# Attention decode kernel on one core: the closing wait for the two output stores moved from SyncE to ScalarE

**Chip and metric.** One core of one Trainium2 chip. The metric is the device time of one execution in microseconds (us), as a median of several executions.

## The reference

A grouped-query attention block with a full key and value cache, for 32 sequences of 4 new positions:

```python
B, Sq, D = 32, 4, 1024
Hq, Hkv, Sk, Dh = 32, 4, 2048, 128
q = (x @ wq).reshape(B, Sq, Hq, Dh).transpose(0, 2, 1, 3)
k = repeat(k_cache, Hq // Hkv, axis=1);  v = repeat(v_cache, Hq // Hkv, axis=1)
p = softmax(einsum("bhqd,bhkd->bhqk", q, k) * Dh ** -0.5)
o = einsum("bhqk,bhkd->bhqd", p, v)
return o.transpose(0, 2, 1, 3).reshape(B, Sq, Hq * Dh) @ wo      # all bfloat16
```

The output is 128 rows by 1024 columns of bfloat16, 256 KB. The inputs are 151 MB.

## The kernel before

Everything up to the last matmul is loads and compute that the change does not touch. What counts is the end. The result lies in PSUM, where the last matmuls write it, in three column ranges; VectorE copies the first and the third to SBUF, ScalarE the second. Two DMAs store it: SyncE issues the left half, ScalarE the right half.

```python
for j, eng in enumerate(("dve", "act", "dve")):
    copy(eng, *COLS[j], j)
for j, (n0, n1, waits) in enumerate(((0, NA, (0,)), (NA, D, (1, 2)))):
    p.dma(("sp", "act")[j], lambda e, n0=n0, n1=n1: e.dma_start(out_flat[:, n0:n1], y_sb[:, n0:n1]),
          [("oe", i) for i in waits], ("out", j), f"s_o{j}")
# ... cut ...
with nc.Block() as block:          # line 499: each engine's stream; closes with a barrier of all engines
    # ... cut: the five engines' streams ...

for j in range(2):                 # after the block
    s, n = p.at["out", j]
    nc.sync.wait_ge(sems[s], n)    # line 523
```

Each store has its own semaphore (`s_o0`, `s_o1`; 114 and 115 in the trace), a counter that is updated 16 times as the store lands: from 360.096 to 360.273 us, and from 360.562 to 360.744. No other instruction of the program waits for the stores: SyncE leaves the block's barrier at 359.709 us, the later store lands at 360.744.

## Time and profile before

| | kernel before |
|---|---|
| time, median of 3 runs | 362.17 us (362.14 to 362.23) |
| span in the profile, first to last instruction | 360.8 us |
| data moved | 151.66 MB, 420 GB/s |
| later store: issue, last landing | 358.976, 360.744 us |
| closing wait on SyncE | 360.761 to 360.789 us |

The span covers the program's own instructions. The time has 1.3 us more (362.09 in the profiled run, for a span of 360.789). What follows the program has no row in any view of the profile, but the trace still holds the times at which semaphores were updated. Semaphore 2 is named by no instruction of the program, and no record says what updates it. Its updates after the block's barrier, from 359.995 to 362.219 us, I number 1 to 18: they come as two groups of nine, which I call passes. Where I say "the record of semaphore 2", this list is meant.

### The profile page before, as it was taken

The numbers are of one execution on the slowest core, as the hardware profiler recorded it, in microseconds if no ns is written. First come the engines' busy times: TensorE is split into PE (matmuls) and PEld (weight loads), VectorE is DVE, ScalarE is ACT, GpSimd is POOL, SyncE is SP. The second block draws the span as 40 slices with busy tenths as digits, with TensorE's granted clock in tenths as the row PEclk, the third lists the DMA queues.
The fourth block names the chain that finished last, engine by engine and source line by source line (L and its number), as shares of the span: only waits on it lengthen the run. The fifth ranks groups of instructions, "written<-read, shape, count | busy, mean of one in ns | idle before, by whom it ended". The sixth has DMA issues, their size and how long they took to land. (4 is left out here: it accounts for less than half of the span.)

```text
span 360.8 us, 6251 instructions
## 1 busy us (share of the span) xinstructions
PE 307.6 (85%) x3034; PEld 147.0 (41%) x2340; DVE 269.5 (75%) x171; ACT 102.8 (28%) x110; POOL 165.9 (46%) x262
## 2 busy tenths in 40 slices
PE   1988788999999999988999888888888898889896
PEld 1002000445444554444444444443333444448721
DVE  0018799999899888879999888888888888865601
ACT  1014222333333333333333333323222233333100
POOL 8002055255555555554455444455555554444100
DMA  8999999999999999999999999999999999999996
GB/s 323 432 434 431 421 429 432 429 417 432 428 423 425 432 431 427 424 432 431 423 427 432 430 423 429 431 432 423 429 431 432 423 429 431 429 425 431 413 417 243
DMA packets 12251, 151.66 MB, mean 420 GB/s; under 512 B 1360, under 2 KB 2128, under 8 KB 2768
## 3 DMA queue, kind: packets, MB, share of 16 engines
q1 hardware_dynamic: 12096, 151.39, 99.1%
q8 instruction: 6, 0.10, 0.1%
q10 hardware_dynamic: 144, 0.13, 0.1%
q14 instruction: 5, 0.04, 0.0%
HBM read 151.26 MB, written 0.26 MB: 420 GB/s over the span
## 5 line engine op out<-in xcount | busy, mean ns | idle before, releaser
L328 DVE STREAM_TRANSPOSE KT_sb<-big 128x2048 f32<-128x2048 f32 x64 | 146.6, 2293 | 16.3 <-DMA big<-in_k_cache_dram 16.3
L354 ACT ACTIVATE P_sb<-ps_s,negmx 128x2048 bf16<-128x2048 f32 x32 | 82.2, 2569 | 184.7 <-DVE negmx L350 184.7
L16 PE MATMUL ps_s<-KT_sb,QD_sb 128*128 128x512 bf16 x384 | 103.7, 377 | 0.0
L385 POOL COPY PD_sb<-PT_sb 32x1024 f32<-32x1024 f32 x62 | 64.3, 1036 | 63.1 <-PE ps_r L394 60.2
L385 POOL COPY big<-PT_sb 32x1024 f32<-32x1024 f32 x61 | 63.2, 1036 | 58.6 <-PE ps_r L394 55.8
L350 DVE TENSOR_REDUCE negmx<-ps_s 128x1 f32<-128x2048 f32 x32 | 73.2, 2287 | 12.4 <-PE ps_s L16 10.8
L394 PE MATMUL ps_r<-big 128*128 128x128 bf16 x1024 | 59.8, 219 | 11.6 <-PEq L85 11.6
L394 PE MATMUL ps_r<-big,PD_sb 128*128 128x128 bf16 x1024 | 59.8, 219 | 9.9 <-PEq L85 9.8
L394 PEld LDWEIGHTS ps_r<-big 128*128 128x128 bf16 x1024 | 57.9, 98 | 22.3 <-issue 21.9
L394 PEld LDWEIGHTS ps_r<-big,PD_sb 128*128 128x128 bf16 x1024 | 58.0, 98 | 21.1 <-issue 20.6
L341 PE MATMUL ps_s<-KT_sb,QD_sb 128*128 128x512 bf16 x128 | 48.3, 377 | 18.1 <-PEq L85 18.1
L341 PEld LDWEIGHTS ps_s<-KT_sb,QD_sb 128*128 128x128 bf16 x128 | 12.3, 96 | 102.8 <-issue 102.8
L363 DVE STREAM_TRANSPOSE PT_sb<-P_sb 128x1024 f32<-128x1024 f32 x32 | 39.8, 1245 | 16.0 <-ACT P_sb L354 16.0
L318 POOL COPY QD_sb<-QT_sb 32x64 f32<-32x64 f32 x128 | 29.6, 231 | 46.1 <-DVE QT_sb L297 20.5
L16 PE MATMUL ps_r<-ident 128*128 128x384 bf16 x173 | 33.3, 325 | 0.0
L366 PEld LDWEIGHTS ps_r<-ssum,permf 128*128 128x128 f32 x64 | 11.9, 187 | 24.8 <-issue 23.1
L403 ACT ACTIVATE QT_sb<-ps_r,rinv 128x128 bf16<-128x128 f32 x32 | 11.8, 368 | 29.6 <-PE ps_r L394 27.3
L279 DVE TENSOR_SCALAR KT_sb<-ps_r 128x512 bf16<-128x512 f32 x2 | 1.3, 688 | 20.1 <-PE ps_r L263 20.1
L420 PE MATMUL ps_s<-big,KT_sb 128*128 128x512 bf16 (+1 forms) x34 | 12.5, 375 | 1.9 <-DMA big<-in_wo_dram 1.0
L434 DVE CAST P_sb<-ps_s 128x512 bf16<-128x512 f32 (+1 forms) x2 | 1.1, 542 | 15.2 <-PE ps_s L420 15.2
L16 PE MATMUL ps_s<-big,KT_sb 128*128 128x224 bf16 (+1 forms) x62 | 12.0, 272 | 0.0
L252 PE MATMUL ps_r<-ident 128*128 128x384 bf16 x32 | 10.3, 322 | 0.0
(41 smaller groups left out, 85.8 us busy)
## 6 DMA issues: line engine op xcount, KB each, us to landing
big<-in_k_cache_dram SPq DMA_DIRECT2D x32, 2048.0 KB, 18.5
big<-in_v_cache_dram SPq DMA_DIRECT2D x32, 2048.0 KB, 22.1
big<-in_wq_dram SPq DMA_DIRECT2D x4, 2048.0 KB, 14.0
big<-in_wo_dram SPq DMA_DIRECT2D x6, 1024.0 KB, 22.9
big<-in_wo_dram SPq DMA_DIRECT2D x2, 512.0 KB, 24.4
big<-in_wo_dram SPq DMA_DIRECT2D x2, 256.0 KB, 22.6
big<-in_wo_dram SPq DMA_DIRECT2D x4, 128.0 KB, 17.5
P_sb<-in_x_dram SPq DMA_DIRECT2D x1, 256.0 KB, 2.7
```

What stands on the lines that cost most here:

```text
L16: return eng.add_instruction(mybir.InstMatmult(name=nc.get_next_instruction_name(), engine=eng.engine, start_tensor_calc=start, stop_tenso ...
L318: p.op("pool", lambda e, s=src, d=dst: e.tensor_copy(d, s), waits if g == 0 else [("pt", i - 2)] * (g == 1 and i > 1), ("qd", i) if g == G ...
L328: p.op("dve", lambda e, s=src, d=dst: e.transpose(d, s), waits, ("kt", i, c), gives="t_kt" if c else None)
L341: mm = lambda e, a_=(out_, lhsT, rhs), f=first, l=last: e.matmul(a_[0], lhsT=a_[1], rhs=a_[2], start=f, stop=l, skip_group_check=True)
L350: p.op("dve", lambda e: e.tensor_reduce(negmx[:, i % 4:i % 4 + 1], ps_s[:, :], AX.X, ALU.max, negate=True), [("qk", i)], ("negmx", i))
L354: p.op("act", lambda e: e.activation(P_sb[:, :, :, :].rearrange("p t r w -> p t w r"), ps_s[:, :].rearrange("p (t w r) -> p t w r", w=2, r=R),
L363: p.op("dve", lambda e: e.transpose(dst, src), [("exp", i)], ("pt", i))
L366: p.op("pe", lambda e: e.matmul(ring[(i if i == L else i // 2 * 2) % 4][:, 510 + i % 2:511 + i % 2], lhsT=permf[:, :], rhs=ssum[:, i % 4:i ...
L385: p.op("dve" if i >= B - 2 and g < i - B + 4 else "pool", lambda e, s=src, d=dst: e.tensor_copy(d, s), [free] * (g == 0 or i >= B - 2) + [ ...
L394: p.op("pe", lambda e: e.matmul(buf[:, 0:Dh], lhsT=pd_of(i)[:, t // 2, :, :, :, t % 2].rearrange("p x g q -> p (x g q)"), rhs=big[:, slot_ ...
L403: p.op("act", lambda e: e.activation(dst, src, ACT.Copy, scale=rinv[:, i % 4:i % 4 + 1]), [("pv", i), ("rinv", i)], ("o", i))
L420: mm = lambda e, a=(out_, lhsT, rhs): e.matmul(a[0], lhsT=a[1], rhs=a[2], start=(u == 0), stop=(u == Hq - 1), skip_group_check=True)
```

## The change

The intent is to let the engine that issued the last store be the one that sees it land, and to let SyncE end with the block's barrier.

```diff
         for j in range(2):
             s, n = p.at["out", j]
-            nc.sync.wait_ge(sems[s], n)
+            nc.scalar.wait_ge(sems[s], n)
```

## The prediction

> **What bounds the kernel now.** I read the page from the top for the bound of the whole, then the chain that ended last for the end of it, and then only the last 3 us, because the diff touches nothing earlier. Kernel before, page, the shares of the span and the DMA rows:

> ```profile
> span 360.8 us, 6251 instructions
> PE 307.6 (85%) x3034; PEld 147.0 (41%) x2340; DVE 269.5 (75%) x171; ACT 102.8 (28%) x110; POOL 165.9 (46%) x262
> DMA  8999999999999999999999999999999999999996
> DMA packets 12251, 151.66 MB, mean 420 GB/s; under 512 B 1360, under 2 KB 2128, under 8 KB 2768
> ```

> The DMA engines are at 90% or more in all but the first and last slice, and 151.66 MB at 420 GB/s is 361 us: the kernel lasts as long as its loads. The diff moves no byte of them. What it can change is the end, where the loads are over. Kernel before, chain of waits that ended last in order of time, its last links (start us, duration us):

> ```profile
> 324.86 27.93 DMA big<-in_wo_dram
> ...
> 357.36 0.45 PE ps_s L420 x2
> 357.81 0.02 issue
> 357.83 1.06 DVE P_sb L434 x2
> ```

> The last weights land, the last matmuls run, the result is copied out of PSUM. The stores come after this list. Kernel before, timeline of the last microseconds:

> ```profile
> 358.40 0.41 ACT L432 ACTIVATE P_sb<-ps_s 128x288 bf16<-128x288 f32 x1 [16.11 <-PE ps_s L420]
> 358.55 0.35 SPq L439 DMA_DIRECT2D out_dram<-P_sb  x1
> 358.98 0.37 ACTq L439 DMA_DIRECT2D out_dram<-P_sb  x1
> ```

> SyncE issues the left half at 358.55, ScalarE the right half at 358.98. Then comes the block's closing barrier and the wait that the diff moves. Kernel before, instructions of the barrier's line 499 and of the wait's line 523 (ns, then start us):

> ```profile
> L499 ACTq DRAIN  x1: 152/152/152, 359.4 to 359.4; - x1
> L499 POOLq EVENT_SEMAPHORE  x2: 17/17/17, 359.6 to 359.6; - x2
> L499 SPq EVENT_SEMAPHORE  x1: 17/17/17, 359.7 to 359.7; - x1
> L499 ACTq EVENT_SEMAPHORE  x1: 17/17/17, 359.7 to 359.7; - x1
> L523 SPq EVENT_SEMAPHORE  x1: 28/28/28, 360.8 to 360.8; - x1
> ```

> The reader is to see that every engine leaves the barrier at 359.7, that SyncE and ScalarE leave it together, and that the single instruction on line 523 (both waits in one) starts at 360.8 and is the last of the span. What it waits for stands in the waits of the SyncE queue (total us, times, longest us) and in the DMA issues (KB, us to landing):

> ```profile
> SPq L523 <- DMA out_dram<-P_sb: 1.0, 1, 1.0
> out_dram<-P_sb SPq DMA_DIRECT2D x1, 128.0 KB, 1.7
> out_dram<-P_sb ACTq DMA_DIRECT2D x1, 128.0 KB, 1.8
> ```

> 358.98 plus 1.8 is 360.8: the later store, ScalarE's, ends the wait. To the nanosecond, the trace's records have the last of the 16 updates of SyncE's store's semaphore at 360.273, that of ScalarE's store at 360.744, and the wait at 360.761 to 360.789.

> [...] 16 updates for the second store, from 360.562 to 360.744, and the wait passes 17 ns after the sixteenth. [...]

> [...] the wait has 28 ns although its engine was free at 359.709.

> [...] The views of the profile stop at the span's end, but the trace's list of semaphore updates goes on[...]. Semaphore 2 is updated at 359.995, 360.029, 360.239 and 360.283, then nothing for 628 ns, then at 360.911, 360.954, 360.992, 361.027 and 361.075[...]; then nine updates more from 361.863 to 362.219.

> **The change part by part.** It removes from SyncE one two-condition wait that is reported with 28 ns. It adds the same to ScalarE, still after the block, so still after the barrier. No data moves and no store is issued at another time: the two issues and the barrier all come before it.

> Inside the span: ScalarE leaves the barrier at 359.714 (SyncE 359.709), over 1 us before the last landing, so its wait is reached in time and passes at 360.744 + 0.017 = 360.761. Its length I take from ScalarE's own one-condition barrier wait, 17 ns, up to SyncE's 28. So the span ends at 360.778 to 360.789: a change of -11 to 0 ns. I take -0.01 us.

> After the span: here the two engines may differ. Of the nine updates of the closing pass, four come before SyncE was free and the fifth 122 ns after its wait ended. So SyncE is fifth[...], 360.911 to 361.075 = 164 ns. ScalarE is one of the first four. Which one, no view says; I read second (PE, ScalarE, GpSimd, VectorE, SyncE)[...].

> If ScalarE waits as second, three upward steps and the turn come after it. The second closing pass, which nothing delays in the middle, gives their sizes: 361.897, 361.936, 361.979, 362.002 upward is 39 + 43 + 23 = 105 ns, the turn to 362.100 is 98 ns, the way down to 362.219 is 38 + 34 + 47 = 119 ns. Together 322 ns, against 164 now: +158 ns. I assume that ScalarE also needs SyncE's 122 ns from its wait to its update. Sum: -11 + 158 = +0.15 us.

> Does the timed interval hold that pass? The time of the profiled run is 362.09 us for a span of 360.8, so 1.3 us lie outside the span. The whole distance from the span's end to the last update is 362.219 - 360.789 = 1.43 us, so the closing passes are the likely place. That it is counted is a choice of mine, made at about three in four.

> **The rivals.** One: nothing at all moves, 362.17 us, because the time stops before the pass, or because the pass is reordered so that ScalarE costs nothing. For it speaks that every view of the profile gives the same end to both kernels; against it the 628 ns gap, which shows that the pass does wait for the engine that waits.

> Two: it gets faster. The intent may be that the engine that issued the last store also sees it land earliest, and that SyncE is free sooner. Against it: 1.0 us of SyncE's last wait is spent on the landing and only 17 ns pass between the sixteenth update and the wait's start; that 17 and the 11 ns of the shorter instruction are all that could be saved, 362.14 us at best. SyncE being free at 359.7 starts nothing, since nothing of the kernel is left.

> Three: the wait slips into the block's barrier, so that all engines are held until 360.78. From the end of ScalarE's drain (359.540) to its release (359.714) is 0.17 us, so this would cost about 0.2 us: 362.4 us. The diff leaves the lines after the block, and I put this at one in twenty.

> Four: ScalarE is at another place in the pass. As fourth it would leave one step up, the turn and the way down, 23 + 98 + 119 = 240 ns, so +76 - 11 = +0.07 us; as first some 34 ns more than as second, so +0.18 us. Either stays far inside 2%, which is 7.2 us.

> **Range and chances.** Centre: 362.17 + 0.15 = 362.32, pulled toward 362.17 by the one in four that the pass isn't counted: 362.17 + 0.75 x 0.15 = 362.28. The runs of before spread by 0.09 us, on one chip[...]. So 362.0 to 362.6 should hold it 8 times in 10. No path leads to 7 us either way, as the wait has all of 1.0 us: faster by over 2% 0.005, within 2% 0.99, slower by over 2% 0.005.

> **What would show it.** Right: the last instruction of the span is one ScalarE event wait on line 523, at 360.8, after ScalarE's barrier instruction at 359.7; SyncE's last is the barrier's; the stores land in 1.7 and 1.8 us as before; the span stays within 0.05 us apart from the noise of the loads; in the semaphore records the pass has its gap after the first update instead of the fourth, and about 320 ns from the second update to the ninth. Wrong: a span shorter or longer by over 0.2 us with the same store times, a barrier release after 360 us (rival three), the gap elsewhere (rival four), or stores that land at another time, which would say that the waiting engine matters to the transfer.

-11 ns for the wait's instruction and +158 ns for the updates (322 from the second update to the ninth, less 164 from the fifth to the ninth) are 147 ns, +0.15 us: 362.32 us, and 362.28 with the pull. "Upward", "turn" and "way down", like the "up", "turn", "down" and "hops" of the expectations, are names for the steps between updates 1 and 5, 5 and 6, 6 and 9; no record shows which engines make the last four. That the waiting engine has no say in the landing was not shown at that time; the ten profiled runs below have 1.7 and 1.8 us whichever waits.

## The result

| | before | after |
|---|---|---|
| time, median of 6 runs, us | 362.17 (362.13 to 362.24) | 362.32 (362.24 to 362.39) |
| ratio | | 1.0004, 95% interval 0.9991 to 1.0017 |
| profiled run: time, span end, us | 362.09, 360.789 | 362.35, 360.877 |

A ratio is the mean time of one kernel's runs over that of the other's of the same rounds, so it is not quite the ratio of the medians. By the rule of 2% the two are the same, and the interval does not exclude that they are equal. The six times of each, however, barely touch, and the records of the trace, which are finer than the times, show a difference.

First the views. Kernel after, instructions of line 523 and of the barrier's line 499, to be held against the same lines of before:

```profile
L499 SPq EVENT_SEMAPHORE  x1: 17/17/17, 359.7 to 359.7; - x1
L499 ACTq EVENT_SEMAPHORE  x1: 17/17/17, 359.7 to 359.7; - x1
...
L523 ACTq EVENT_SEMAPHORE  x1: 38/38/38, 360.8 to 360.8; - x1
```

The wait stands on ScalarE (ACTq), SyncE's last is the barrier, and it is still one instruction, of 38 ns where SyncE's had 28. Kernel after, timeline and DMA issues of the two stores (start us and duration us; KB and us to landing):

```profile
358.60 0.35 SPq L439 DMA_DIRECT2D out_dram<-P_sb  x1
359.02 0.37 ACTq L439 DMA_DIRECT2D out_dram<-P_sb  x1
```

```profile
out_dram<-P_sb SPq DMA_DIRECT2D x1, 128.0 KB, 1.7
out_dram<-P_sb ACTq DMA_DIRECT2D x1, 128.0 KB, 1.8
```

The stores take as long as before. Both are issued 0.05 us later than in the profile of before, as are the copies out of PSUM ahead of them (VectorE starts its first at 357.88 against 357.83), so this shift arises ahead of the lines that the change touches. By the records the later store then took 1.793 us to its last landing, against 1.768. The two together put the last landing 74 ns later (360.818 against 360.744), and with it 74 of the 88 ns by which the span got longer. To be free of that, everything below is counted from the last landing.

The record of semaphore 2, its first nine updates after the program (us) and the steps between them (ns):

```
before:  359.995  360.029  360.239  360.283 | 360.911  360.954  360.992  361.027  361.075
            34      210       44      628        43       38       35       48
after:   360.045 | 360.991  361.030  361.073  361.096  361.196  361.234  361.268  361.315
            946       39       43       23      100       38       34       47
```

The bar marks where the pass waited for the engine with the closing wait. The first update behind the bar I count as that engine's own; the experiments below test this. Before, four updates were done while SyncE waited, and four steps followed SyncE's own. After, one update was done while ScalarE waited, and seven steps followed ScalarE's own. From the last landing to the ninth update, in four terms:

| ns | before | after | difference |
|---|---|---|---|
| last landing to end of the wait | 45 | 59 | +14 |
| end of the wait to that engine's own update | 122 | 114 | -8 |
| own update to the ninth | 164 | 324 | +160 |
| sum | 331 | 497 | +166 |

The +160 has, but for 2 ns, two parts: the three steps from the second update to the fifth (105 ns), and the step after the fifth, which is 100 ns where the fifth came 23 ns after the fourth and 43 where it came 628 ns after it. Why these two differ, no run here shows.

From the ninth update to the eighteenth and last it is 1144 ns before and 1147 after: what is lost in the first pass is not given back.

### The profile page after: what moved, and what is told of

It reads as the page before. It is cut to its first block, busy times and chain, and to the rows that moved or that the text cites. A ratio compares the mean times of both kernels' runs of the same rounds, so it can differ in the third digit from the quotient of the medians.

```text
span 360.9 us, 6251 instructions
## 1 busy us (share of the span) xinstructions
PE 307.1 (85%) x3034; PEld 147.0 (41%) x2340; DVE 269.4 (75%) x171; ACT 102.6 (28%) x110; POOL 165.3 (46%) x262
## 2 busy tenths in 40 slices
DMA  8999999999999999999999999999999999999996
DMA packets 12251, 151.66 MB, mean 420 GB/s; under 512 B 1360, under 2 KB 2128, under 8 KB 2768
## 5 line engine op out<-in xcount | busy, mean ns | idle before, releaser
L420 PE MATMUL ps_s<-big,KT_sb 128*128 128x512 bf16 (+1 forms) x34 | 12.5, 375 | 2.0 <-DMA big<-in_wo_dram 1.1
L434 DVE CAST P_sb<-ps_s 128x512 bf16<-128x512 f32 (+1 forms) x2 | 1.1, 541 | 15.3 <-PE ps_s L420 15.3
## 6 DMA issues: line engine op xcount, KB each, us to landing
big<-in_wo_dram SPq DMA_DIRECT2D x4, 128.0 KB, 17.5
```

The costliest lines, as they stand in the source:

```text
L420: mm = lambda e, a=(out_, lhsT, rhs): e.matmul(a[0], lhsT=a[1], rhs=a[2], start=(u == 0), stop=(u == Hq - 1), skip_group_check=True)
```

## The experiments

**Waits crossed.** ScalarE gets a wait too, but for the store that lands first.

```diff
-            nc.sync.wait_ge(sems[s], n)
+            (nc.scalar, nc.sync)[j].wait_ge(sems[s], n)
```

> ScalarE waits for SyncE's store, which landed 0.47 us earlier in the kernel before (360.273 against 360.744), SyncE for ScalarE's. Theory of the pass [...]: ScalarE is free at about 360.29 and passes on at about 360.4, before SyncE is, so the gap before the fifth update stays and the ninth comes 164 ns after SyncE's: time 362.17, as the kernel before, within 0.05. Rival, a wait on ScalarE costs by itself, its own bookkeeping or its longer instruction (38 against 28 ns): 362.3, as the kernel after. Rival, scatter: cannot be told from the first here.

Measured: 362.08 us against 362.11 of the kernel before in the same rounds, ratio 1.0000 (0.9986 to 1.0013). Instructions of line 523 in this kernel:

```profile
L523 ACTq EVENT_SEMAPHORE  x1: 17/17/17, 360.3 to 360.3; - x1
L523 SPq EVENT_SEMAPHORE  x1: 17/17/17, 360.8 to 360.8; - x1
```

ScalarE has a wait and a store, as in the kernel after, and it costs nothing: its update comes at 360.442, two more follow in 38 and 44 ns, and the pass then waits 379 ns for SyncE, from whose update the ninth follows in 164 ns. The rival "ScalarE's wait costs by itself" falls for a wait with one condition; the next run takes up the two conditions. From the last landing to the ninth update it is 320 ns, 11 fewer than before, which is what SyncE's instruction saves with one condition instead of two (17 ns against 28). The times cannot show 11 ns.

**Each engine waits for its own store.** The same, the other way round.

```diff
-            nc.sync.wait_ge(sems[s], n)
+            (nc.sync, nc.scalar)[j].wait_ge(sems[s], n)
```

> Each engine waits for the store that it issued itself: SyncE for the earlier one, ScalarE for the later one. Theory of the pass: ScalarE is last to be free and stands second, so as the kernel after, 362.32, with the ninth update about 324 ns after ScalarE's. Rival, that the double condition of one instruction on ScalarE is what costs (38 against 28 ns, and 14 ns more from landing to the wait's end): 362.17 to 362.2. Rival, scatter: 362.17 plus or minus 0.1, whatever the kernel.

Measured: 362.31 us against 362.11, ratio 1.0003 (0.9989 to 1.0017).

```profile
L523 SPq EVENT_SEMAPHORE  x1: 17/17/17, 360.4 to 360.4; - x1
L523 ACTq EVENT_SEMAPHORE  x1: 17/17/17, 360.9 to 360.9; - x1
```

These are the two instructions of the crossed kernel with their semaphores exchanged, and so with the other engine last (start us and the engine in each line). The last landing is 475 ns before the ninth update, 155 more than with the waits crossed; 323 of the 475 lie after ScalarE's own update. The rival of the double condition explains 22 ns of the kernel after (475 against 497), not the rest.

**Waits on TensorE**, by the theory the first of the pass.

```diff
-            nc.sync.wait_ge(sems[s], n)
+            nc.tensor.wait_ge(sems[s], n)
```

> Both waits on TensorE, which the theory places first. Theory of the pass: all eight hops follow the wait, 35 + 39 + 43 + 23 up, 98 turn, 38 + 34 + 47 down = 357 ns against 164, so +0.19 us if TensorE needs SyncE's 122 ns from wait to update: 362.36; up to 362.48 if it needs the 240 ns that lie between its release from the barrier and its first update. In the records all nine updates come after the wait. Rival, ScalarE's own cost: 362.17. Rival, scatter: 362.17 plus or minus 0.1.

Measured: 362.40 us (362.32 to 362.47) against 362.11, ratio 1.0008 (0.9994 to 1.0021). The instruction ends at 360.747 and all nine updates come after it, from 360.947 to 361.305, 358 ns; 357 was expected. From the wait's end to the first update it is 200 ns, between the two values allowed for. The wait in this kernel:

```profile
L523 PEldq EVENT_SEMAPHORE  x1: 51/51/51, 360.7 to 360.7; - x1
```

**Waits on VectorE**, by the theory the fourth.

```diff
-            nc.sync.wait_ge(sems[s], n)
+            nc.vector.wait_ge(sems[s], n)
```

> Both waits on VectorE, which the theory places fourth. Theory of the pass: 23 + 98 + 119 = 240 ns from its update to the ninth, against 164, so +0.08 us: 362.25, between before and after; three updates before the gap, six after. Rival, ScalarE's own cost: 362.17. Rival, scatter: 362.17 plus or minus 0.1. The time alone may not tell these apart, the place of the gap does.

Measured: 362.30 us (362.30 to 362.40) against 362.11, ratio 1.0006 (0.9992 to 1.0019). The gap stands where it was expected, after the third update, and 241 ns lie between VectorE's update and the ninth (240 expected). The time was expected lower, at 362.25, because I had given VectorE SyncE's own costs: its wait ends 78 ns after the landing, not 45, and 161 ns follow to its update, not 122. So the place in the pass is not the whole cost; these 33 and 39 ns come on top. Line 523 shows a part of it, 49 ns for the instruction:

```profile
L523 DVEq EVENT_SEMAPHORE  x1: 49/49/49, 360.8 to 360.8; - x1
```

**Waits on GpSimd**, by the theory the third.

```diff
-            nc.sync.wait_ge(sems[s], n)
+            nc.gpsimd.wait_ge(sems[s], n)
```

> Both waits on GpSimd, which the theory places third. Theory of the pass: 43 + 23 + 98 + 119 = 283 ns from its update to the ninth. Its own time from the wait to its update is not known: as SyncE's 122 ns it would give +0.12 us, 362.29; if it is the 572 ns that lie between its last barrier instruction and its update in the kernel before, +0.57 us, 362.74. Two updates before the gap, seven after. Rival, ScalarE's own cost: 362.17. Rival, scatter: 362.17 plus or minus 0.1.

Measured: 362.72 us (362.63 to 362.87) against 362.16, ratio 1.0015 (1.0001 to 1.0029), the upper of the two cases. The gap stands after the second update, and 285 ns lie between GpSimd's update and the ninth (283 expected). The rest is GpSimd's own: its wait ends at 360.838 and its update comes at 361.380, 542 ns later. This also fits the odd 210 ns step in the pass of the kernel before: there the third update comes at 360.239, 572 ns after GpSimd's last barrier instruction, and was hidden behind the stores, the later of which landed at 360.744. The view of line 523 shows nothing of it, only a short wait at the usual time:

```profile
L523 POOLq EVENT_SEMAPHORE  x1: 43/43/43, 360.8 to 360.8; - x1
```

**Waits on SyncE, inside the block**, the prediction's third rival made real.

```diff
             def _(eng):
                 p.emit("sp", eng, sems, lead)
+                for j in range(2):
+                    s, n = p.at["out", j]
+                    eng.wait_ge(sems[s], n)
# ... cut ...
-        for j in range(2):
-            s, n = p.at["out", j]
-            nc.sync.wait_ge(sems[s], n)
```

> Both waits on SyncE, but inside the block, ahead of its part of the closing barrier, as the prediction's third rival has it. Theory: the barrier and the first half of the pass no longer run while the store is in flight. Release at 360.79 + 0.12 (SyncE's drain) + 0.17 = 361.08 instead of 359.71; then the slowest of the first four updates, 0.53 us after the release in the kernel before, and 43 + 23 + 98 + 119 = 283 ns: ninth update at 361.89 against 361.075, so +0.8 us: 363.0. Had I taken only the barrier itself, as in the prediction, +0.2: 362.4. No cost of the place: 362.17.

Measured: 363.06 us (362.93 to 363.69) against 362.16, ratio 1.0028 (1.0014 to 1.0041). The wait (line 510 here) now comes ahead of the barrier. By the trace it holds the condition of the later store alone; that of the earlier one sits on a branch of SyncE that follows (line 499, 33 ns), so the edit also splits the wait in two:

```profile
L510 SPq EVENT_SEMAPHORE  x1: 17/17/17, 360.7 to 360.7; - x1
...
L499 SPq COMPARE_BRANCH  x1: 33/33/33, 360.8 to 360.8; - x1
L499 SPq DRAIN  x1: 7/7/7, 360.9 to 360.9; - x1
L499 SPq EVENT_SEMAPHORE  x1: 17/17/17, 361.1 to 361.1; - x1
L499 ACTq EVENT_SEMAPHORE  x1: 17/17/17, 361.1 to 361.1; - x1
```

From the last landing (360.693) to the ninth update (361.918) it is 1225 ns, 894 more than before: 367 to the end of GpSimd's last barrier instruction (34 of them to the end of the wait, 212 more to the end of SyncE's drain), 572 from there to its update, 286 for the rest of the pass. The prediction had counted only the barrier, about 0.2 us. The larger part is that the first updates of the pass, with the 572 ns to GpSimd's, come after the landing and no longer while the store is in flight.

**The kernel after again, and the kernel before against itself**. The edit of the first is the change itself; the second has none.

> The kernel after once more, beside the control on the same chip. Theory of the pass: 362.32, 0.15 above the kernel before, in every round. Scatter: as far from the kernel before as the control is.

> The kernel before against itself, unchanged: ratio 1.0000, difference of the medians under 0.05 us. If it is 0.15, the difference of the kernel after can't be told from scatter by its times.

Measured: after 362.40 us (362.23 to 362.48), ratio 1.0004 (0.9990 to 1.0017); control 362.19 us (362.07 to 362.40), ratio 0.9999 (0.9985 to 1.0012), against 362.16 for the kernel before (362.04 to 362.50). So 0.03 us is what two copies of the same kernel differ by in the median, while single times of the kernel before differ by up to 0.46 us. "0.15 in every round" did not hold: time by time, in the order recorded, after lies 0.02 to 0.29 us above the control, and its lowest time (362.23) is below the highest of before (362.50). The times alone support the difference only by three medians and their sign. The records are unequivocal: from the last landing to the ninth update the control has 331 ns, as the kernel before has, and the repeat of after 497, as the kernel after has.

Where the pass waits, in the steps between its nine updates (ns; the long step, between bars, ends with what I count as the update of the engine that waited last; in the crossed kernel the first step, 441, is ScalarE's wait for the earlier store):

```
crossed, SyncE last     441    38    44 |  379 |  44    38    34    48
own stores, ScalarE   | 898 |  38    44    23    98    39    35    46
TensorE             (all after the wait)  34    39    43    23   100    38    34    47
VectorE                  35   210 | 744 |  23    98    40    34    46
GpSimd                   34 |1328 |  44    23    98    40    34    46
after again, ScalarE  | 918 |  39    44    23    98    40    34    46
control, SyncE           34   210    44 |  626 |  44    38    34    48
```

The long step ends with the second update for ScalarE, the third for GpSimd, the fourth for VectorE and the fifth for SyncE, and with TensorE all nine come after the wait: the order of the theory.

All of it in one table, in the order of the pass; ns from the records of one profiled run for each kernel (the second runs of before and after give the same sums, 331 and 497), the time's difference from the medians of the same rounds:

| last wait on | wait's length | landing to wait's end | to own update | to the ninth | sum | over before | time over before, us |
|---|---|---|---|---|---|---|---|
| TensorE | 51 | 80 | 200 | 358 | 638 | +307 | +0.29 |
| ScalarE (after) | 38 | 59 | 114 | 324 | 497 | +166 | +0.15; again +0.24 |
| ScalarE, own store only | 17 | 39 | 113 | 323 | 475 | +144 | +0.20 |
| GpSimd | 43 | 68 | 542 | 285 | 895 | +564 | +0.56 |
| VectorE | 49 | 78 | 161 | 241 | 480 | +149 | +0.19 |
| SyncE (before) | 28 | 45 | 122 | 164 | 331 | 0 | 0; control +0.03 |
| SyncE, crossed | 17 | 34 | 122 | 164 | 320 | -11 | -0.03 |

A wait's own length went with its engine and, but for TensorE, with its conditions: 17 ns with one and 28 with two on SyncE, 17 and 38 on ScalarE, 21 (in the barrier) and 49 on VectorE, 17 (in the barrier) and 43 on GpSimd, 51 (in the barrier) and 51 on TensorE. The fifth column falls from one end of the pass to the other. The sums of the five kernels with both conditions on one engine fall with it (638, 497, 480, 331) but for GpSimd's 895, which its fourth column makes. No version beats the kernel before by anything that the times can show; the crossed one is 11 ns better on the records.

## Why the prediction was right

The time, 362.32 us, is the value of its own sum before the pull toward 362.17, and lies 0.04 us above the centre. With single times scattering as they do, that close an agreement of the medians is partly luck; what was tested is the terms.

- Loads set the time, and the change touches only the end: right. Both pages have 151.66 MB at 420 GB/s and the DMA engines at 90% or more in 38 of 40 slices; the stores land in 1.7 and 1.8 us as before.
- The change inside the span, -11 to 0 ns: wrong in sign and of no weight. ScalarE's instruction took 38 ns, not 17 to 28, and started 21 ns after the last landing, not 17, so the term is +14 ns. The repeat has the same 38 ns. A wait with one condition had indeed 17 ns on ScalarE; the second condition costs it 21 ns, and SyncE 11.
- SyncE's 122 ns for ScalarE's own update: 114 measured, -8 ns where 0 was assumed.
- The pass, +158 ns: +160 measured. That ScalarE stands second was only inferred, and what it was inferred from is cut, as no trace shows it. So the right place was in part luck. The gap after the first update shows it, and the four other engines' gaps show the rest of the order.
- The shape of the pass: nine updates, and the five places of the gap, are what the traces show. An order of engines for updates 6 to 9 is not shown, and no term of the sum needs it, as the steps themselves are measured (119 ns together in the second pass of the kernel before, 38, 34 and 47 in the first of the kernel after).
- The pass is counted in the time, put at three in four: shown. In all ten profiled runs the eighteenth update comes 112 to 136 ns after the span's start plus the run's time, although the last landing to the eighteenth varies from 1465 to 2371 ns.
- Rival one (nothing moves) falls by the records; by the times it would stand. Rival two (faster) falls. Rival three did not happen in the kernel after; made on purpose it costs 0.9 us, so its term of 0.2 us was mis-sized: it left out the pass (572 + 286 ns), and the stretch to the end of SyncE's drain (212 ns). Rival four falls by the place of the gap.

What stays open: why 542 to 572 ns lie between GpSimd's last instruction and its update, which no record here shows, and why the steps between the ninth and the tenth update are 788 to 790 ns in seven profiled runs and 814 to 820 in three, one of them the control.

## What to carry to other kernels

In this kernel the last wait is followed by updates of semaphore 2 that depend on which engine is released last: 164 ns of them remain after SyncE's own, 324 after ScalarE's, 358 after TensorE's. So in a kernel that ends like this one put it on the engine whose own update came last of the five (SyncE here), and behind the block's closing barrier, not inside: the barrier and the first four updates are then hidden under the store's flight, which was worth 0.9 us here (362.16 against 363.06). Which engine waits makes no difference to when the store lands (1.7 and 1.8 us in all ten profiled runs), and ScalarE gained nothing by waiting for the store that it had issued itself (475 ns, against 320 with SyncE waiting for it). No run issued a store from another engine, so what that would do is not shown. Effects of 0.15 us in 362 cannot be read from a handful of times (those of the kernel before differ by up to 0.46 us); count them from a common event in the records of one run.
